# Weights converted from the first attention on, an output product behind the next norm, and norms half a pair ahead

**The chip, the cores and the metric.** One core of one Trainium2 chip. The metric is the device time of one execution in microseconds (us), the slowest core's, which is the only one here. All runs quoted are in the fast state. Kernels sent together ran on the same chip beside runs of the kernel before, and are compared with those.

## The reference

Eight sequences of 448 tokens: attention with 12 heads of 64 channels, q and k normed by their root mean square, then a feed-forward layer with SwiGLU over 768 channels and 1536 hidden units. Cut to what matters:

```python
q_n, k_n = rmsnorm(q, g_q), rmsnorm(k, g_k)
attn = softmax(q_n @ k_n.T / sqrt(64)) @ v            # 8 x 12 heads, 448 x 64
x  = attn.transpose(0, 2, 1, 3).reshape(3584, 768)
xn = x / sqrt(mean(x * x) + 1e-6) * rms_g
g  = xn @ w_gate
out = (g * sigmoid(g) * (xn @ w_val)) @ w_out         # weights come as 64-bit floats
```

## The kernel before

Two heads make a pair, six pairs a sequence, 48 pairs in all. One loop iteration `g` scores pair `g`, brings its exponentials to the values of pair `g - 1`, and transposes q and k of pair `g + 1`. (The code, and some of the recorded texts, call a transpose a turn too; in the text here a turn is a turn of the conversion, explained next.) TensorE (PE) fills the gaps of attention with the gate, value and output products of the sequence before. The product is a two by two block scheme with seven products, so sums of weight blocks are needed.

The weights come as 64-bit floats. A conversion **turn** takes one 128 x 384 block through ScalarE (ACT, two steps), GpSimd (POOL, a clamp), DVE (two integer steps) and GpSimd again (the join). The result is used by sequence 0 and stored for the other seven. There are 72 blocks, and a turn works on four of them in different steps:

```python
def split(raw):                       # turn n works on block n - 2 here
    nc.scalar.activation(top, hi, ACT.Abs)
    nc.scalar.activation(lo, lo, ACT.Copy, scale=2.0**-29)
    nc.gpsimd.tensor_scalar(top, top, 122879.99, 2.0**-15, ALU.min, ALU.max)      # the clamp
def join(lo, hi, top, dst):           # and on block n - 3 here
    nc.vector.tensor_scalar(top, top, 3, 0x3FFFFFF8, ...)                         # DVE step 1
    nc.vector.scalar_tensor_tensor(top, hi, -(2**30), top, ...)                   # DVE step 2
    nc.gpsimd.tensor_tensor(dst, top, lo, ALU.add)                                # the join
def convert():
    ... keep (store) what the turn before joined; join block n - 3;
    ... DVE subtractions for the sums of block n - 4; split block n - 2; load block n
```

The order of the loop body decides what each engine does in what order:

```python
for g in range(NG + 1):
    load_pair(g + 2)                  # q and k, on the same queue as the conversion's loads and stores
    pe(lambda: score(g, (0, 1)))
    squares(g + 2, 0)                 # ACT square; DVE sum one PE item later
    if solo: convert()                # solo: attention without products beside it (pairs 0 to 5)
    fill()                            # products, each followed by convert()
    pe(lambda: turn(g + 1, 0))
    ...
    squares(g + 2, 1)                 # two PE items later: GpSimd's root and q's norm
    pe(lambda: values(g - 1))         # bank ps_m
    load_v(g + 2)
    ...
    pe(lambda: sums(g - 1))           # DVE: reciprocal, then x = values * reciprocal, frees ps_m
    fill()
    pe(lambda: turn(g + 1, 1))        # bank ps_m again
    ...
```

`ps_m` is a single PSUM bank, shared by values and transposes; the scores have four banks and the products three.

Of the kernel before, what the change touches and what calls it, by code (L numbers as in the profile page):

```python
# [8 lines left out]
F32 = mybir.dt.float32  # L9
# [325 lines left out]
def safe_scores(  # L335
# [24 lines left out]

    RING, NH = 24, 14
    const, small = pool("c_const", 1), pool("c_small", 4)
    qk_pool, v_pool, qn_pool, qkT_pool = pool("c_qk", 3), pool("c_v", 3), pool("c_qn", 1), pool("c_qkT", 2)
    e_pool, tmp, y_pool = pool("c_e", 12), pool("c_tmp", 1), pool("c_y", 2)
    x_pool, s_pool, h_pool, w_pool = pool("c_x", 4), pool("c_xs", 3), pool("c_h", NH), pool("c_w", RING)
    raw_pool, cv_pool = pool("c_raw", 4), pool("c_cv", 2)
    scratch = pool("c_dram", 1, space=DRAM)
# [23 lines left out]
    def load_pair(g):  # L391
        if g >= NG:
            return
        b, hp = divmod(g, NPAIR)
        hs = slice(2 * hp, 2 * hp + 2)
        qk = st["qk", g] = qk_pool.tile([P, 2, 2 * NT * D], F32, name="qk")

        for h in range(2):
            nc.sync.dma_start(out=qk[:, 1].rearrange("p (t h d) -> p h t d", h=2, d=D)[:, h],  # L399
                              in_=k[b, 2 * hp + h].rearrange("(p t) d -> p t d", t=NT))  # L400
        nc.sync.dma_start(out=qk[:, 0].rearrange("p (h n) -> p h n", h=2), in_=q[b, hs].rearrange("h (p t) d -> p h (t d)", t=NT))

# [11 lines left out]
    def squares(g, i):  # L414

        if g >= NG:
            return
        n = 2 * NT
        if i == 0:
            st["ms", g] = small.tile([P, 2 * n], F32, name="ms")  # L420
        ms = st["ms", g]
        sq = tmp.tile([P, n * D], F32, name="sq", tag="sq", bufs=1)
        nc.scalar.activation(sq, st["qk", g][:, i], ACT.Square)  # L423

        def reduce():
            nc.vector.tensor_reduce(out=ms[:, i * n:(i + 1) * n], in_=sq.rearrange("p (n d) -> p n d", d=D), axis=AX_X, op=ALU.add)  # L426

        after(1, reduce)
        if i == 1:
            after(2, lambda: rms_qk(g))  # L430
            after(2, lambda: norm_q(g))

    def rms_qk(g):
        ms = st.pop(("ms", g))
        nc.gpsimd.tensor_scalar(ms, ms, 1.0 / D, 1e-6, ALU.mult, ALU.add)  # L435
        rs = st["rs", g] = small.tile([P, 4 * NT], F32, name="rs")
        nc.gpsimd.tensor_tensor(rs, ms, mhalf[0:P, :], ALU.pow)  # L437

# [58 lines left out]
    def sums(g):  # L497
# [25 lines left out]
        for c in range(NT):  # L523
            for j in range(2):
                st.pop(("e", g, c, j))
        for key in ("qk", "v", "qkT", "rs"):
            st.pop((key, g))
# [13 lines left out]
    def norm_x(b):  # L541
# [5 lines left out]
        for hp in range(NPAIR):  # L547
            x = st["x", b, hp // 3][:, hp % 3, :]
            nc.vector.scalar_tensor_tensor(x, x, rg[:, hp:hp + 1], ps[:, 0:S], ALU.mult, ALU.mult)

        a = st["left", b] = {f"A{r + 1}{h + 1}": st["x", b, h][:, :, r * HT:(r + 1) * HT] for r in range(2) for h in range(2)}
        for h in range(2):
# [20 lines left out]

    made = []

    def block():
        t = h_pool.tile([128, 512], F32, name="h")[:, 0:BW] if len(made) < NH else w_pool.tile([128, BW], F32, name="wt")
        made.append(False)
        return t, len(made) - 1

    def room(n):

        return all(made[i - RING] for i in range(len(made), len(made) + n) if i - RING >= NH)

# [38 lines left out]
    def keep(key):  # L623
        t = st[key][0]
        if key[0] == "wo":
            nc.sync.dma_start(out=kept_o[key[3], key[2]], in_=t)  # L626
        else:
            nc.sync.dma_start(out=kept[key[2], ORDER.index(key[3]), key[4]], in_=t)

    def convert(upto=None):  # L630
# [7 lines left out]
        if 0 <= n - 3 < len(pieces):  # L638
            key = pieces[n - 3][0]
            st[key] = block()  # L640
            join(*st.pop(("cv", n - 3)), st[key][0])
            if "B12" not in key:
                store.append(key)
        if 0 <= n - 4 < len(pieces) and pieces[n - 4][0][0] == "w":
            _, _, fp, name, w = pieces[n - 4][0]
            sums = {"B12": (("T1", "B12", "B11"), ("T2", "B22", "T1"), ("T3", "B22", "B12")), "B21": (("T4", "B21", "T2"),)}
            for to, plus, minus in sums.get(name, ()):
                key = ("w", 0, fp, to, w)
                st[key] = block()
                nc.vector.tensor_tensor(st[key][0], st["w", 0, fp, plus, w][0], st["w", 0, fp, minus, w][0], ALU.subtract)  # L650
                store.append(key)
            if name == "B12":
                made[st.pop(pieces[n - 4][0])[1]] = True
        if 0 <= n - 2 < len(pieces):
# [13 lines left out]
    def used(key):  # L668

        made[st.pop(key)[1]] = True  # L670
        upto = min(at_use[key] + 1 + AHEAD, len(uses))
        while asked["n"] < upto and room(1) and turn_of["n"] == len(pieces) + 5:
            key = uses[asked["n"]]
            asked["n"] += 1
            t, i = st[key] = block()
            nc.sync.dma_start(out=t, in_=kept_o[key[3], key[2]] if key[0] == "wo" else kept[key[2], ORDER.index(key[3]), key[4]])


    def product(b, fp, left, right, onto=None):
# [3 lines left out]
        for w in range(2):  # L683
            wt = st["w", b, fp, right, w][0]
            for c in range(3):
# [5 lines left out]
    def quad(b, fp):  # L691
# [33 lines left out]
        def p2():  # L725
            product(b, fp, "A12", "B21", onto=bank["a"])
            for fc in (fp, fp + NFP):
                st["h", b, fc] = h_pool.tile([128, 512], F32, name="h")
                if b % 2:

                    nc.gpsimd.tensor_copy(st["h", b, fc][:, 0:64], st.pop(("h", b - 1, fc))[:, S - 64:S])
            hand(bank["a"][:, 0:HT], bank["a"][:, HT:S], rows(fp)[:, 0:HT])
# [24 lines left out]
    def project_out(b, n, i, part, last):  # L757
# [5 lines left out]
        for fc in range(part * each, (part + 1) * each):  # L763
            nc.tensor.matmul(ps, lhsT=st["h", b, fc][:, i * 128:(i + 1) * 128], rhs=st["wo", b, n, fc][0],  # L764
                             start=(fc == 0), stop=(fc == NFC - 1))
            if last:
                used(("wo", b, n, fc))
        if part < OUT_PARTS - 1:
            return
# [13 lines left out]

    def ffn_items(b):

        items = []
        for fp in range(NFP):
            items += [(6 * HT, 8 * (fp + 1) + 5, fn) for fn in quad(b, fp)]
        tiles = 3 + b % 2
        for n in range(2):  # L790
            for i in range(tiles):
                for part in range(OUT_PARTS):
                    items.append((NFC // OUT_PARTS * HALF, 8 * NFP + NFC * (n + 1) + 4,
                                  lambda a=(b, n, i, part, i == tiles - 1): project_out(*a)))
        return items


    AHEAD, LEFT, SLOTS = 20, 7, 27
    todo, part = [], {"all": 0.0, "spent": 0.0, "slot": 0}

    def fill(n=None):

        if n is None:
            part["slot"] += 1
            upto = part["all"] * min(part["slot"] / SLOTS, 1.0)
            n = 0
            while n < len(todo) and part["spent"] + todo[n][0] / 2 < upto:
                part["spent"] += todo[n][0]
                n += 1
        for _ in range(n):  # L810
            if not todo:
                pe(idle)
                continue
            _, turns, fn = todo.pop(0)
# [7 lines left out]

    def begin(b):
        items = ffn_items(b)
        part.update(all=float(sum(c for c, _, _ in items[:-LEFT])), spent=0.0, slot=0)
        todo.extend(items)


    for g in range(2):
        load_pair(g)  # L830
    for g in range(2):
        load_v(g)
    ident = const.tile([128, 128], F32, name="ident")
    make_identity(nc, ident)
    ones = const.tile([128, D], F32, name="ones")
    nc.vector.memset(ones, 1.0)
    mhalf = const.tile([128, 4 * NT], F32, name="mhalf")
    nc.gpsimd.memset(mhalf, -0.5)
    gq = const.tile([128, 1], F32, name="gq")
    gk = const.tile([128, 1], F32, name="gk")  # L840
    for a in range(2):
        rows = slice(a * D, (a + 1) * D)
        nc.scalar.dma_start(out=gq[rows, :], in_=g_q.rearrange("(p o) -> p o", o=1))
        nc.scalar.dma_start(out=gk[rows, :], in_=g_k.rearrange("(p o) -> p o", o=1))
    rg = const.tile([128, NDC], F32, name="rg")
    nc.scalar.dma_start(out=rg, in_=moe_rms_g.rearrange("(c p) -> p c", p=128))
    row = const.tile([1, 2, D], F32, name="row")
    nc.scalar.dma_start(out=row[:, 0, :], in_=g_q.rearrange("(o d) -> o d", o=1))
    nc.scalar.dma_start(out=row[:, 1, :], in_=g_k.rearrange("(o d) -> o d", o=1))
    gqk = const.tile([128, 1], F32, name="gqk")  # L850
# [13 lines left out]
    squares(0, 1)  # L864
    pe(idle)
    squares(1, 0)
    pe(idle)
    squares(1, 1)
    pe(lambda: turn(0, 1))
    bound()  # L870
    pe(lambda: turn(0, 0))
    for g in range(NG + 1):
        b, hp = divmod(g, NPAIR)
        load_pair(g + 2)
        solo = alone(g)
        if g < NG:
            pe(lambda: score(g, (0, 1)))
        squares(g + 2, 0)
        if solo:
            convert()  # L880
# [3 lines left out]
        if solo:  # L884
            pe(lambda: turn(g + 1, 1))
        squares(g + 2, 1)
        if g:
            pe(lambda: values(g - 1))
        load_v(g + 2)
        if solo:  # L890
# [4 lines left out]
        if solo:  # L895
            convert()
            continue
        end = hp == 0
        fill(2 if end else None)
# [4 lines left out]
        if end:  # L904
# [4 lines left out]
            fill(len(todo))  # L909
            begin(b - 1)  # L910
        fill()
    fill(len(todo))
    pe(idle)
    pe(idle)
    pe(idle)

# [37 lines left out]
```

## Time and profile before

The median was 1782.95 us. The prediction below shows the windows and the main waits; two more waits are needed later. Columns: engine, waiting line, releaser, then us in total, times and the longest.

```profile
DVE top L604 <- POOL top L599: 60.5, 42, 3.7
...
PE tr L454 <- issue: 12.2, 3, 4.5
```

The first is DVE standing for the clamp before its first step. The second is a transpose on TensorE that waits for nothing that the profile names; by its place I read it as a wait for the free `ps_m` bank (such waits are gone in the run below that gives it another bank).

### The profile page before, as it was taken

Reading aid. Unit: us, or ns where it says so; the run is one execution under the profiler, and the core shown is the slowest. Engines: PE = TensorE matmul, PEld = TensorE weight load, DVE = VectorE, ACT = ScalarE, POOL = GpSimd, SP = SyncE. Lnnn points to the kernel's source line nnn. Section 1 sums busy time; section 2 is a strip of 40 time slices with the busy share of each in tenths; the row PEclk is TensorE's granted clock in tenths of the full one; section 3 lists DMA queues with packets and bytes.
Section 4 is the critical chain, followed back from the end, with each engine's and each line's share of the span. In section 5 each row is a group of like instructions: output and inputs, shape, how many; then the busy total and the mean of one; then the engine's idle time right before and its main releaser. Section 6 shows DMA issues by size and latency. Waiting matters only on the chain.

```text
span 1778.6 us, 21555 instructions
## 1 busy us (share of the span) xinstructions
PE 1679.7 (94%) x7688; PEld 1207.5 (68%) x7688; DVE 728.7 (41%) x1078; ACT 487.3 (27%) x945; POOL 670.4 (38%) x643
## 2 busy tenths in 40 slices
PE   5869777889999999999999999999999999999998
PEld 2337566458875688758885588757885588858975
DVE  2756766544341344324442344324442244323320
ACT  5634344423222223222322232322322222210100
POOL 4665666653333334342333333432433323311000
PEclk9879888899999999999999999999999999999999
DMA  5624565646443445336542355325542264426521
GB/s 134 195 92 133 190 194 182 196 135 200 128 127 94 142 147 151 93 104 193 155 132 87 94 161 165 113 92 185 159 140 73 88 187 137 124 71 190 175 81 46
DMA packets 224841, 243.77 MB, mean 137 GB/s; under 512 B 63957, under 2 KB 221653, under 8 KB 224725
## 3 DMA queue, kind: packets, MB, share of 16 engines
q1 hardware_dynamic: 223616, 242.30, 44.3%
q8 instruction: 63, 1.03, 0.2%
q14 instruction: 54, 0.43, 0.1%
q10 hardware_dynamic: 1108, 0.00, 0.0%
HBM read 209.98 MB, written 32.24 MB: 136 GB/s over the span
## 4 chain that ended last, share of the span: by engine, by line
PE 79%; ACT 0%; DMA 0%; SPq 0%; issue 0%; DVE 0%; ACTq 0%; POOL 0%
PE ff L686 38%; PE ff L764 23%; PE sc L469 7%; PE av L494 7%; PE den L506 2%; PE tr L454 1%; PE rb L545 0%; PE msx L535 0%; ACT qkT L457 0%; DMA qk<-in_q_dram 0%; SPq L399 0%; DVE y L774 0%; ACT top L597 0%; ACT raw L598 0%; SPq L626 0%
## 5 line engine op out<-in xcount | busy, mean ns | idle before, releaser
L686 PE MATMUL ff<-x,wt 128*128 128x224 f32 x2268 | 469.5, 360 | 19.3 <-ACT p L719 17.5
L686 PEld LDWEIGHTS ff<-x,wt 128*128 128x128 f32 x2268 | 431.7, 194 | 52.5 <-issue 39.4
L764 PE MATMUL ff<-wt,h 128*128 128x384 f32 x1344 | 455.7, 492 | 7.6 <-DVE h L709 4.4
L764 PEld LDWEIGHTS ff<-wt,h 128*128 128x128 f32 x1344 | 250.0, 191 | 195.6 <-issue 27.5
L686 PE MATMUL ff<-xs,wt 128*128 128x224 f32 x1692 | 348.9, 356 | 3.5 <-DVE cc L698 3.5
L686 PEld LDWEIGHTS ff<-xs,wt 128*128 128x128 f32 x1692 | 316.3, 191 | 29.3 <-issue 16.4
L473 ACT ACTIVATE e<-sc,rs 112x448 f32<-112x448 f32 x384 | 212.2, 635 | 248.3 <-PE sc L469 237.5
L483 POOL TENSOR_TENSOR es<-es,e 112x448 f32<-112x448 f32 x168 | 189.7, 1140 | 234.4 <-ACT e L473 227.9
L510 DVE RECIPROCAL rd<-den 128x448 f32<-128x448 f32 x48 | 141.9, 2956 | 137.5 <-PE den L506 137.5
L494 PE MATMUL av<-e,vt 112*64 112x448 f32 x768 | 165.6, 576 | 16.4 <-ACT qkT L457 14.0
L469 PE MATMUL sc<-qkT 64*112 64x448 f32 x768 | 173.3, 569 | 0.7 <-ACT qkT L457 0.7
L479 POOL TENSOR_TENSOR es<-e 112x448 f32<-112x448 f32 x84 | 96.6, 1171 | 179.8 <-ACT e L473 179.8
L437 POOL TENSOR_TENSOR rs<-ms,mhalf 112x16 f32<-112x16 f32 x48 | 140.2, 2921 | 4.0
L426 DVE TENSOR_REDUCE ms<-sq 112x8 f32<-112x512 f32 x96 | 65.3, 680 | 184.5 <-ACT sq L423 184.2
L494 PEld LDWEIGHTS av<-e,vt 112*64 112x64 f32 x768 | 54.0, 144 | 105.3 <-issue 88.6
L469 PEld LDWEIGHTS sc<-qkT 64*112 64x112 f32 x768 | 62.3, 175 | 78.0 <-issue 68.8
L435 POOL TENSOR_SCALAR ms<-ms 112x16 f32<-112x16 f32 x48 | 10.2, 212 | 278.4 <-DVE ms L426 277.4
L698 DVE TENSOR_TENSOR cc<-ff,u 128x448 f32<-128x448 f32 x96 | 59.8, 623 | 132.2 <-PE ff L686 132.0
L606 POOL TENSOR_TENSOR wt<-top,raw 128x384 int32<-128x384 int32 x64 | 68.6, 1071 | 92.8 <-DVE top L605 29.5
L522 POOL TENSOR_TENSOR ss<-ss,rd 128x448 f32<-128x448 f32 x40 | 46.3, 1158 | 119.1 <-ACT rd L521 119.1
L423 ACT ACTIVATE sq<-qk 112x512 f32<-112x512 f32 x96 | 60.6, 631 | 61.9 <-DMA qk<-in_q_dram 54.1
L698 DVE TENSOR_TENSOR u<-ff,u 128x448 f32<-128x448 f32 x48 | 29.9, 623 | 106.1 <-PE ff L686 106.1
(67 smaller groups left out, 1073.1 us busy)
## 6 DMA issues: line engine op xcount, KB each, us to landing
wt<-kept SPq DMA_DIRECT2D x588, 192.0 KB, 3.3
wt<-kept_o SPq DMA_DIRECT2D x168, 192.0 KB, 2.5
kept<-wt SPq DMA_DIRECT2D x72, 192.0 KB, 2.3
qk<-in_k_dram SPq DMA_DIRECT2D x96, 112.0 KB, 3.1
qk<-in_q_dram SPq DMA_DIRECT2D x48, 224.0 KB, 3.2
vt<-in_v_dram SPq DMA_DIRECT2D x48, 224.0 KB, 2.7
raw<-in_moe_w_gate_dram SPq DMA_DIRECT2D x24, 384.0 KB, 3.9
raw<-in_moe_w_val_dram SPq DMA_DIRECT2D x24, 384.0 KB, 3.6
```

The costliest lines, as they stand in the source:

```text
L426: nc.vector.tensor_reduce(out=ms[:, i * n:(i + 1) * n], in_=sq.rearrange("p (n d) -> p n d", d=D), axis=AX_X, op=ALU.add)
L437: nc.gpsimd.tensor_tensor(rs, ms, mhalf[0:P, :], ALU.pow)
L469: nc.tensor.matmul(ps[0:P, 0:S], lhsT=qkT[r, 1, c * P:(c + 1) * P], rhs=qkT[r, 0, :], start=True, stop=True)
L473: nc.scalar.activation(e, ps[0:P, 0:S], ACT.Exp, scale=rs[:, n:n + 1])
L479: nc.gpsimd.tensor_tensor(es, st["e", g, 0, j], st["e", g, 1, j], ALU.add)
L483: nc.gpsimd.tensor_tensor(es, es, st["e", g, c, j], ALU.add)
L494: nc.tensor.matmul(av[j * D:(j + 1) * D, 0:S], lhsT=vt[:, j, c, :], rhs=st["e", g, c, j], start=(c == 0), stop=(c == NT - 1))
L510: nc.vector.reciprocal(rd, den[:, 0:S])
L606: nc.gpsimd.tensor_tensor(dst.bitcast(I32), top, lo, ALU.add)
L686: nc.tensor.matmul(bank[:, w * HT:(w + 1) * HT], lhsT=wt[:, c * 128:(c + 1) * 128], rhs=x[:, c, :], start=onto is None and w == c == 0, st ...
L698: nc.vector.tensor_tensor(add[name], ps[:, 0:S], add[other], ALU.add)
L764: nc.tensor.matmul(ps, lhsT=st["h", b, fc][:, i * 128:(i + 1) * 128], rhs=st["wo", b, n, fc][0], start=(fc == 0), stop=(fc == NFC - 1))
```

## The change

The intent was to win from the time that TensorE loses before 397 us (the prediction puts it at 128 us): to start conversion with the first attention, to spread its turns one behind each product, to have norms ready earlier, and to give the norm between two sequences something to hide behind. Its core:

```diff
+    free_w = [slots.tile([128, BW], F32, name=f"w{i}") for i in range(NW)]     # a list of free places
     def room(n):
-        return all(made[i - RING] for i in ...)          # a ring: freed in order only
+        return len(free_w) + max(len(free_h) - 4, 0) >= n
-    raw_pool, cv_pool = pool("c_raw", 4), pool("c_cv", 2)
+    raw_pool, cv_pool = pool("c_raw", 4), pool("c_cv", 3)
...
+    def out_items(b): ...
     def begin(b, slots):
-        items = ffn_items(b)                             # gate and value, then output product
+        items = (out_items(b - 1) if b else []) + gate_value_items(b)
...
     squares(0, 1)
+    pe(lambda: turn(0, 1))
+    convert()
+    convert()
...
-        solo = alone(g)                                  # pairs 0 to 5
+        solo = g <= NPAIR                                # pairs 0 to 6
         load_pair(g + 2)
         pe(lambda: score(g, (0, 1)))
         squares(g + 2, 0)
+        squares(g + 2, 1)
...
-        squares(g + 2, 1)
         if g: pe(lambda: values(g - 1))
+        if g == NPAIR + 1: pe(lambda: rms_x(0))          # the first seam
```

At the start a dummy square draws the table load forward, q is loaded before k, and pair 0's roots are computed in two halves.

> **What bounds the kernel now.** I read the windows view first, cut at the places where the program changes its work: start, attention alone (pairs 0 to 5), the first seam (norm of sequence 0), gate, value and output products of sequence 0 beside attention and weight conversion, the rest.
>
> ```profile
> 0.00:15.00 15.00, 1.98 (x8) 1.32 (x8) 4.09 (x11) 4.25 (x6) 6.32 (x12) 1.00 0.70 179
> 15.00:97.00 82.00, 68.09 (x306) 27.74 (x308) 47.68 (x64) 52.46 (x101) 50.57 (x48) 0.90 0.54 160
> 97.00:137.00 40.00, 25.25 (x96) 14.55 (x96) 22.14 (x28) 9.70 (x18) 21.56 (x19) 0.70 0.23 72
> 137.00:397.00 260.00, 212.47 (x908) 150.21 (x907) 160.39 (x254) 103.35 (x209) 166.19 (x175) 0.91 0.54 171
> 397.00:1778.00 1381.00, 1371.92 (x6375) 1013.67 (x6374) 494.38 (x725) 317.56 (x613) 425.73 (x391) 1.00 0.43 131
> ```
>
> After the window, the columns are PE, weight loads, DVE, ACT, POOL, then granted clock. From 397 us on TensorE is busy 99% at full clock and nothing can be won but matmuls; the change removes none. Before 397 us, PE is idle 89 us and its clock is reduced.
>
> I priced the work by start-to-start times of the later timeline: a gate/value product of 12 matmuls 2.28 us, an output item of 8 matmuls 2.60, an attention pair 9.06 (1.69 + 1.69 scores, 3.1 values, 0.9 sums, 0.8 turns, switches), 2.3 more where the sums are on PE. Two sequences in the later part then cost 84 x 2.275 + 42 x 2.58 + 12 x 9.06 = 408 us, the period that the timeline has (811.25 to 1219.46). Work done by 397 us at that price: 12.5 pairs' parts, 42 products and 18 output items, some 268 us. **The loss is about 128 us**: 14 in the start, 24 in attention alone (82 - 58), 23 at the seam (40 - 17), 66 in the long window (260 - 194). That is the most that can be won.
>
> Who holds PE there? The waits of PE and ACT:
>
> ```profile
> PE tr L454 <- POOL qn L441: 22.1, 5, 7.0
> PE ff L686 <- ACT p L719: 17.5, 4, 5.9
> PE av L494 <- ACT qkT L457: 14.0, 9, 4.5
> ACT top L597 <- POOL wt L606: 86.7, 46, 4.9
> ACT sq L423 <- DMA qk<-in_q_dram: 54.1, 20, 3.9
> ```
>
> PE waits for the normed q, and for ACT copies that are themselves short. ACT is late because, in its order, each conversion's first step (L597) needs the top tile freed by POOL's last step (L606), 87 us in 46 waits. POOL's timeline in a burst shows the cause:
>
> ```profile
> 318.77 1.01 POOL L606 TENSOR_TENSOR wt<-top,raw 128x384 int32<-128x384 int32 x1 [1.22 <-DMA kept_o<-wt]
> 319.74 0.51 POOL L599 TENSOR_SCALAR top<-top 128x384 f32<-128x384 f32 x1
> 321.47 1.00 POOL L606 TENSOR_TENSOR wt<-top,raw 128x384 int32<-128x384 int32 x1 [1.22 <-DMA kept_o<-wt]
> ```
>
> One turn of the conversion is a serial chain: join 1.0, clamp 0.5, DVE's two steps 0.36 + 0.56 and the hand-overs: 321.47 - 318.77 = **2.70 us a turn**. There are 77 turns.
>
> **What the skill says.** "TensorE: Matmul & The Clock Gate", part 1, says that the clock falls to half after an idle window of about 3.4 us and returns after about as long of work. The trace agrees: after 5.89 us idle at 221.93 a product takes 4.39 us, against 2.43, and the granted clock of 220 to 240 us is 0.77. So each PE wait removed returns somewhat more than its length. The same page, section "Architectural detail", calls ACT, DVE and GpSimd strict FIFO; the late ACT copies above fit. "SBUF — State Buffer", "Who interferes with whom", says that a DVE tensor_tensor with both inputs in SBUF contends with GpSimd reads. The trace fits: such subtractions (L650) are 0.55 us at best and 0.80 on average. "ScalarE: Activation LUTs", "What ACT_TABLE_LOAD costs", gives 1283 ns; the trace has 1283.
>
> **The change part by part.** I walked both programs' emission order and counted turns (c), with no time in it.
>
> (1) Start. The dummy Square draws the table load (1.28 us, now at 5.00 behind seven ACT DMA issues) before the data; q is loaded first; pair 0's roots are split, so that q's root has 8 columns. From 16 columns 2.92 and 4 columns 1.02 I estimate 1.65 for 8. q lands about 5, square 0.63, reduce 0.69, POOL 0.2 + 1.65 + 1.04, turns 1.0, copy 0.63: first score near 11.5 in place of 15.2. Loss 14 becomes 10.5.
>
> (2) Attention alone now covers pairs 0 to 6. Turns reached: 22, against 18 at its end before; the list allows no more (34 usable blocks, less a margin of 4). POOL per pair: norms 4.15, ss 1.15, three turns 8.1, less what fits in chain gaps: about 12.5 us; DVE 10.4, PE 10.5. Both roots are emitted half a pair earlier, which removes the qn waits of this stretch (11.2 us). I put 24 us for pairs 0 and 1 (now 26), four of 12.5 (now 14 on average), 14 for pair 6, whose turns share the single ps_m bank: from 11.5 to 99 or so, say 97, against work of 67: loss 19 in place of 24, with a pair and four turns more done.
>
> (3) First seam, now in iteration 7. Same chain (ss add, matmul, root 1.02, matmul, six multiplications 3.64, differences 3.2), one qn wait of 3.9 gone: loss 16 in place of 23.
>
> (4) Sequence 0's products. Before, conversions come in bursts: 3 at each second-half fp, 5 before the output product, 3 in its middle, which PE waits out, since a ring slot frees only in order. Now a slot is taken from whatever is free: one turn follows each product, and the walk shows forced turns only at c62-63 and c73-75. With three top buffers ACT is one turn freer. What stays is POOL's chain. From the seam to the first product of sequence 1: 55 turns x 2.7 = 148, 7.3 pairs x 12.3 (norms 4.15, es adds 6.9, ss 1.15) = 90, less some 35 that fit in gaps, plus 21 for DVE's reciprocals and sums in the chain: **224 to 232 us**. PE's work in the same stretch: 40 x 2.28 + 18 x 2.6 + 7.3 x 9.06 = 204. So POOL stays the bound by a little: loss 28. The same sum for the kernel before gives 229 where 253 was measured; the 24 left over is the alternation of bursts and products, which goes.
>
> Sum of losses: 10.5 + 19 + 16 + 28 = 73.5, against 128: gain 54.
>
> (5) The seam in the later part. Now the last two products of a sequence lie behind the norm, and the output items follow. Three PSUM banks rotate: the first output item takes the bank that the last product still fills, so it waits for its addition on DVE, estimated 0.8 us; and the root has one product (2.3) in place of one output item (2.6) to hide behind, some 0.3. With 7 seams: **loss 7**. The end has more PE work without attention, at the same 100%. Total gain 47: 1783 - 47 = **1736**, which I round to 1737.
>
> **Rivals.** (A) POOL isn't the bound after all, the chain's gaps hold the attention work, and PE runs through: loss in part 4 about 10 and in part 2 about 13, time near 1713. For it: POOL is busy only 64% of 137 to 397. Against: 2.7 us a turn is serial, and POOL's order is unchanged. (B) The chain, not the bursts, is what was measured: 77 turns at the old pace of 3.9 us, output items (2.6 us each 2 turns' worth of chain) waiting in iteration 13, where ten parts meet 13 turns; then the gain is start, seam and one pair, 20 to 25 us: 1760. For it: DVE and POOL are both 62 to 64% busy already and slow each other. Against: PE's named waits there are ACT, at burst positions. (C) Both squares now stand together in ACT's order and may wait for a late k load, holding exps and turns in every iteration; plus seam waits over 3 us that drop the clock: 1775 to 1790. Against: the q load was issued last before, so the old first square already waited for all three loads; at most 3.9 us, and the later part has slack.
>
> **Range and chances.** Centre 1737; A and B lie about 24 us to both sides, so 8 in 10 between 1715 and 1762. The 2% line is 1747. B reaches beyond it, the centre doesn't: faster by over 2% 0.67, within 2% 0.32, slower 0.01.
>
> **What would show it.** First score at 11 to 12.5 us; the first product of sequence 0 near 120 and of sequence 1 near 360 in the timeline; PE waits for ACT p gone, ACT top waits for POOL wt under 30 us; POOL and DVE over 70% busy between; PE busy over 97% afterwards, with some 1 us before the first output item of each seam. Wrong if PE's idle time before sequence 1 stays above 80 us, or if the later part shows waits of several us at its seams.

## The result

The changed kernel took 1783.83 us (1782.27 to 1784.77, 4 runs) against 1783.18 us (1781.13 to 1784.4, 4 runs) of the kernel before in the same rounds: a ratio of 1.0004, 95% interval 0.9987 to 1.0021. **Nothing was won.** Ratios here and below are the mean time of one kernel's fast runs over that of the other's of the same rounds, so they differ a little from the ratio of the medians quoted. The outputs are correct.

The windows of the changed kernel, with the columns and the last four of the stretches that the prediction used for the kernel before (us, then PE, weight loads, DVE, ACT, POOL, granted clock, DMA share, GB/s):

```profile
15.00:97.00 82.00, 70.02 (x304) 28.68 (x304) 54.47 (x75) 52.86 (x105) 56.33 (x55) 0.92 0.61 190
97.00:137.00 40.00, 23.40 (x96) 9.21 (x96) 13.22 (x16) 10.83 (x21) 25.83 (x24) 0.74 0.29 84
137.00:397.00 260.00, 210.13 (x918) 149.36 (x919) 177.99 (x260) 106.33 (x215) 170.40 (x173) 0.91 0.50 154
397.00:1778.00 1381.00, 1374.03 (x6356) 1016.34 (x6354) 488.56 (x716) 309.08 (x594) 415.92 (x381) 1.00 0.44 132
```

The last row is as before. Between 137 and 397 us TensorE did 918 matmuls in place of 908. Cut instead where the program's own work changes (first score, head of iteration 7, second product of sequence 0, first product of sequence 1):

```profile
10.14:120.20 110.06, 85.25 (x362) 34.20 (x362) 61.42 (x88) 62.39 (x122) 73.40 (x72) 0.88 0.59 178
120.20:145.02 24.82, 18.27 (x75) 10.54 (x74) 16.23 (x19) 7.10 (x15) 11.58 (x10) 0.79 0.11 33
145.02:414.54 269.52, 220.88 (x962) 152.26 (x960) 174.84 (x251) 105.32 (x214) 174.60 (x175) 0.92 0.51 157
414.54:1781.30 1366.76, 1356.49 (x6290) 1007.67 (x6288) 483.88 (x712) 307.37 (x591) 411.72 (x378) 1.00 0.44 131
```

At the prediction's prices, the first row holds 67 us of work, the second a pair and two products (9.06 + 4.56), the third 204. So the losses are 43, some 11 and 65.5, with 10 for the start: **about 129 us, where 73.5 was predicted and 128 was there before.** Of the third row's 65.5 us, 48.6 are idle time of TensorE (269.5 less 220.9); the other 17 or so are work that took longer than priced, at a granted clock of 0.92. The last row needs care: the kernel before spends 1382 us after its first product of sequence 1, but has two pairs more to do there (it has done 208 of the score matmuls by then, the changed kernel 240, and a pair has 16). That is 16.4 us at the prediction's price of a pair without its switches (8.18) and 18.1 with them (9.06), so the later part of the changed kernel is 1 to 3 us longer.

The waits of the changed kernel:

```profile
ACT sq L423 <- DMA qk<-in_q_dram: 62.6, 21, 6.7
DVE top L621 <- POOL top L616: 60.8, 37, 5.4
ACT top L614 <- POOL w L623: 24.1, 10, 5.3
PE tr L460 <- issue: 20.3, 5, 8.7
PE tr L460 <- POOL qn L447: 11.8, 6, 4.2
PE ff L703 <- ACT p L736: 4.6, 1, 4.6
```

The waits that the prediction went after did fall: ACT for the join from 86.7 to 24.1, products for ACT from 17.5 to 4.6, transposes for the normed q from 22.1 to 11.8. In their place stand longer waits for the q load, and for the `ps_m` bank (20.3 against 12.2). DVE waits for the clamp as long as before.

### The profile page after: what moved, and what is told of

Its sections match the earlier page's. It is cut to its first block, busy times and chain, and to the rows that moved or that the text cites. A ratio compares the mean times of both kernels' runs of the same rounds, so it can differ in the third digit from the quotient of the medians.

```text
span 1781.3 us, 21585 instructions
## 1 busy us (share of the span) xinstructions
PE 1682.9 (94%) x7688; PEld 1206.0 (68%) x7688; DVE 739.9 (42%) x1078; ACT 486.8 (27%) x946; POOL 676.6 (38%) x645
## 3 DMA queue, kind: packets, MB, share of 16 engines
q8 instruction: 63, 1.03, 0.2%
## 4 chain that ended last, share of the span: by engine, by line
PE 78%; POOL 2%; ACT 1%; issue 1%; DMA 0%; DVE 0%; SPq 0%; ACTq 0%; POOLq 0%
PE ff L703 37%; PE ff L783 24%; PE av L500 6%; PE sc L475 6%; PE den L512 2%; PE tr L460 1%; POOL es L489 1%; PE rb L551 0%; POOL rs L545 0%; ACT e L479 0%; ACT qkT L463 0%; DMA qk<-in_k_dram 0%; DMA raw<-in_moe_w_out_dram 0%; ACT top L614 0%; DVE xs L566 0%
## 5 line engine op out<-in xcount | busy, mean ns | idle before, releaser
L703 PE MATMUL ff<-x,w 128*128 128x224 f32 x2256 | 470.5, 360 | 7.4 <-ACT p L736 4.6
L703 PEld LDWEIGHTS ff<-x,w 128*128 128x128 f32 x2256 | 424.2, 193 | 58.7 <-issue 32.1
L783 PE MATMUL ff<-w,h 128*128 128x384 f32 x1344 | 452.1, 492 | 5.5 <-DVE h L726 5.5
L783 PEld LDWEIGHTS ff<-w,h 128*128 128x128 f32 x1344 | 252.0, 191 | 191.9 <-issue 25.3
L703 PE MATMUL ff<-xs,w 128*128 128x224 f32 x1716 | 350.5, 354 | 3.5 <-DVE cc L715 1.9
L703 PEld LDWEIGHTS ff<-xs,w 128*128 128x128 f32 x1716 | 321.9, 190 | 12.7 <-issue 5.6
L489 POOL TENSOR_TENSOR es<-es,e 112x448 f32<-112x448 f32 x168 | 195.4, 1173 | 264.7 <-ACT e L479 258.1
L443 POOL TENSOR_TENSOR rs<-ms,mhalf 112x16 f32<-112x16 f32 (+1 forms) x49 | 141.6, 2890 | 4.1
L623 POOL TENSOR_TENSOR w<-top,raw 128x384 int32<-128x384 int32 x69 | 73.1, 1060 | 102.0 <-issue 29.7
L423 ACT ACTIVATE sq<-qk 112x512 f32<-112x512 f32 x96 | 57.8, 638 | 74.6 <-DMA qk<-in_q_dram 62.6
L795 DVE COPY y<-ff 128x384 f32<-128x384 f32 x24 | 13.3, 554 | 152.7 <-PE ff L783 152.7
```

Of the source, the lines that this page charges most:

```text
L443: nc.gpsimd.tensor_tensor(st["rs", g][:, cols], ms, mhalf[0:P, cols], ALU.pow)
L489: nc.gpsimd.tensor_tensor(es, es, st["e", g, c, j], ALU.add)
L623: nc.gpsimd.tensor_tensor(dst.bitcast(I32), top, lo, ALU.add)
L703: nc.tensor.matmul(bank[:, w * HT:(w + 1) * HT], lhsT=wt[:, c * 128:(c + 1) * 128], rhs=x[:, c, :], start=onto is None and w == c == 0, st ...
L783: nc.tensor.matmul(ps, lhsT=st["h", b, fc][:, i * 128:(i + 1) * 128], rhs=data(("wo", b, n, fc)), start=(fc == 0), stop=(fc == NFC - 1))
```

## The experiments

Seventeen kernels ran. To place a gain, I use two landmarks of the timeline: the start of the first product of sequence 0 (P0) and of sequence 1 (P1). In the changed kernel P0 is at 137.8 and P1 at 414.5 us, so P0 to P1 is 276.7, and the rest after P1 is 1366.8. That rest was between 1366.8 and 1368.2 us in every variant of the changed kernel that kept its order and was looked at, so everything below happens before P1.

### The ceiling: no conversion at all

The arithmetic and the 64-bit loads are taken out; each place is filled by a plain load (wrong on purpose).

```diff
-            join(*st.pop(("cv", n - 3)), data(key))
+            load_plain(n - 3, data(key))
-            st["cv", n - 2] = split(st.pop(("raw", n - 2)))
-            st["raw", n] = load_raw(pieces[n][1])
```

> The changed kernel with the conversion's arithmetic taken out (each block is filled by one plain load of other finite data; wrong result on purpose; stores, sums of weights, products and order kept). If the loss before sequence 1 (some 130 us in both kernels) is conversion work and its waits on ACT, DVE and POOL: first product of sequence 1 comes near 320 us in place of 414, and the time falls to 1690 to 1705. If it is the attention's own chain (norms, sums on POOL, one bank for turns and values): over 1750.

Measured: 1720.62 us, ratio 0.9643 (0.9627 to 0.9659). P0 is at 117.2 and P0 to P1 takes 234.8. So conversion costs the changed kernel 20 us before P0 and 42 between, and the place to look is right. The same edit on the kernel before:

> The kernel before with the conversion's arithmetic taken out as in e1 (wrong result on purpose). e1 came to 1721, so 63 us of the changed kernel's loss is conversion and some 67 is not. If conversion costs the kernel before more, as the prediction had it (bursts), and the rest is alike: about 1718 to 1725 here too, so the change has bought nothing on either count. If this comes clearly below 1715, the change has added waits of its own that have nothing to do with conversion; clearly above 1735, it has removed such.

It gave 1755.76 us, ratio 0.9846 (0.9828 to 0.9864), but isn't a clean ceiling: the plain load is asked for only at the join, and at the bursts of that kernel the engines wait for it to land (output products wait 8.8 us in 6 for such loads in its trace). The recorded expectation took over 1735 us as a sign that the change had removed waits that have nothing to do with conversion; with these loads in the way I draw nothing from it.

### Attention alone: the load queue

One round of the attention-only stretch, from the timeline of the changed kernel. First the queue that issues the loads and stores (start, us, queue, line, transfer), from one q load to the next:

```profile
84.89 0.48 SPq L397 DMA_DIRECT2D qk<-in_q_dram  x1
...
91.63 0.43 SPq L605 DMA_DIRECT2D raw<-in_moe_w_val_dram  x1
99.03 0.80 SPq L645 DMA_DIRECT2D kept<-h  x2
99.91 0.40 SPq L605 DMA_DIRECT2D raw<-in_moe_w_gate_dram  x1
100.37 0.53 SPq L397 DMA_DIRECT2D qk<-in_q_dram  x1
```

Then ACT, waiting for that q load, and GpSimd in the same round:

```profile
88.58 0.63 ACT L423 ACTIVATE sq<-qk 112x512 f32<-112x512 f32 x1 [5.30 <-DMA qk<-in_q_dram]
```

```profile
94.00 2.91 POOL L443 TENSOR_TENSOR rs<-ms,mhalf 112x16 f32<-112x16 f32 x1
96.99 1.04 POOL L447 TENSOR_TENSOR qn<-qk,rs 112x512 f32<-112x512 f32 x1
97.99 1.01 POOL L623 TENSOR_TENSOR h<-top,raw 128x384 int32<-128x384 int32 x1
```

It closes a circle of 15.5 us: q load at 84.89, square at 88.58, root at 94.00 and norm, then the join that stands behind them in GpSimd's order, then the store of a joined block at 99.03, and behind that store, in the queue's order, the next q load at 100.37. The queue was quiet from 92 to 99 us. The Trainium skill, "DMA: Bandwidth & Descriptors", section "Anatomy of one DMA — SWDGE (gpsimd) path", says that DMA engines don't wait on semaphores, and that the wait happens on the issuing sequencer before dispatch. (The section is about DMAs that GpSimd issues; these are issued by SyncE.) The trace agrees: the queue's own waits have, over the whole execution, 100.2 us in 25 for a join ahead of a store. A load with nothing to wait for is held by the store ahead of it. The test asks for q and k a pair earlier:

```diff
-        load_pair(g + 2)
+        load_pair(g + 3)          # and load_pair(2) before the loop
```

> The changed kernel with q and k loaded one pair earlier (pair g + 3 in place of g + 2 at the head of iteration g; same buffers). Theory 'load loop': the q and k loads stand in the SP queue behind raw loads that wait for POOL's join, POOL's join stands behind the norms, and the norms wait for the loads, 15.5 us around, which is the pace of attention alone (14.8 to 15.7 us a pair). Then ACT's 48 us of waits for the q load go, attention alone runs at 12 us a pair, and the time is 1745 to 1765. Theory 'conversion chain' (POOL and DVE hand each piece to and fro in order): the pace stays near 15 us, time over 1775.

Measured: 1767.75 us, ratio 0.9908 (0.9891 to 0.9924), against 1.0004 unedited: 17 us won. ACT's wait for q falls from 62.6 to 1.9 us, and P0 comes 13 us earlier, at 124.7. On the kernel before:

> The kernel before with q and k loaded one pair earlier, nothing else. ACT waits for the q load 24 us before 400 us there (48 in the changed kernel). If the load loop holds it too: 1765 to 1775. If the loop is what the change itself tightened: within 4 us of 1783.

1774.54 us, ratio 0.995 (0.9932 to 0.9967): 9 us. But in its trace P0 comes only 1.6 us earlier (128.3 against 129.9), and P0 to P1 is 3.9 us shorter, so in that kernel the late load cost little of the attention-only stretch. The circle as the limit of that stretch is shown for the changed kernel alone.

### Pair 6 alone: one bank

The changed kernel gives pair 6 to the attention-only stretch too, but the transposes in that iteration (those of pair 7) are in the single bank `ps_m`, which the values use too. That iteration took 26 us. In the changed kernel's timeline of TensorE:

```profile
108.15 1.01 PE L460 MATMUL tr<-ident,qk 112*128 112x112 f32 x4 [9.42 <-ACT qkT L463]
```

The transpose of k waits 9.42 us for ACT's copy of the transpose of q out of the same bank; ACT itself stood for a q load. Using the then idle product banks:

```diff
-        ps = (ps_f if alone(g - 1) else ps_m).tile(...)
+        ps = (ps_f if g - 1 <= NPAIR else ps_m).tile(...)
```

> The changed kernel with the turns of pair 7, which stand in the last iteration of attention alone, in the three ff banks (unused there) in place of the single bank that turns and values share. Theory 'single bank': the 9.4 us wait of the k turn for the q turn's copy in that iteration goes, and the time falls by 6 to 10 us, 1774 to 1778. If ACT is late there only because it waits for the q load (6.7 us just before), the wait moves to the next instruction and the time stays within 3 us of 1784.

1778.77 us, ratio 0.9972 (0.9955 to 0.9989): 6 us, P0 at 131.3. The opposite cure is to leave pair 6 out of the stretch, as before:

```diff
-        solo = g <= NPAIR
+        solo = g < NPAIR          # the first seam goes back to the general one
```

> The changed kernel with attention alone for pairs 0 to 5 only and sequence 0's products begun after the seam of iteration 6, as before; 21 turns done there; everything else of the change kept. Theory: the extra pair alone (26 us for 9.7 us of matmuls, against 15 for the others) cost what the start and the spreading won; then this is 8 to 15 us faster, 1769 to 1776. Rival: the time is set by the conversion's pace, so that where the products begin does not matter: within 4 us of 1784.

1794.18 us, ratio 1.0061 (1.0043 to 1.0078): slower by 10 us. P0 comes 8 us earlier, at 129.9, but P1 comes 8 us later, at 423.0. So the extra pair isn't what cost the gain. Why it is worth its time stays open: at P0 that run has only one conversion turn fewer behind it (22 raw loads asked for, against 23), and the edit also moves the seam into the general order of the loop. Between P0 and P1 it has at most one pair more to do (half a pair's scores, one pair's values), 9 us or less; at least 7 of the 16.4 us more are not explained.

### Products of sequence 0: were the bursts a cost?

The prediction's step 4 says that bursts of turns cost 24 us, beside the turns themselves. Bring bursts back:

```diff
             pe(fn)
-            convert()
+            if turns > 8 * NFP + 5:       # only behind output items
+                convert()
```

> The changed kernel with one line of the change's effect undone: a gate or value product is no longer followed by a conversion turn of its own, so turns come in bursts of 7 or 8 before the first product of each block and 11 before the output product, as in the kernel before or worse. The prediction's step 4 said that such bursts alone cost about 24 us of the loss beside the products of sequence 0. Theory of the prediction (bursts cost time of their own): 1800 us or more, with TensorE standing at the bursts. Rival (the sum of DVE's and GpSimd's work and their in-order waits for one another set the pace of this stretch, so the placing of the turns in it is nearly free): within 6 us of the changed kernel's 1784, and the idle time of TensorE before sequence 1's first product stays at about 130 us.

1839.46 us, ratio 1.03 (1.028 to 1.032). P0 to P1 is 333.9, 57 us more, and TensorE stands at the bursts, as the waits of TensorE show:

```profile
PE ff L703 <- DVE w L667: 44.6, 8, 11.8
```

These bursts (7 or 8 turns) are larger than those of the kernel before, so 57 is no measure of what those cost. But the rival, that placing is free, has fallen: **spreading the turns is worth time against such bursts**. That something else in the change takes it back is the guess that the next runs test.

### What took it back: the early norms

```diff
         squares(g + 2, 0)
-        squares(g + 2, 1)
         ...
+        squares(g + 2, 1)                 # back where it was
         if g: pe(lambda: values(g - 1))
```

> The changed kernel with the k square of pair g+2 back where it was, half an iteration later (the root and q's norm follow it). If emitting the norms half a pair ahead is worth what the prediction's step 2 took for it (11 us of GpSimd waits), the time rises by 5 to 12 us, to 1789 to 1796. If instead the round that sets the pace of the attention-only stretch is q load, square, reduction, root, join, kept store, next q load, then asking for the norms half a pair earlier only makes ACT and DVE stand earlier for a load that isn't there, and the time is unchanged or falls: 1776 to 1784.

1769.14 us, ratio 0.9911 (0.9891 to 0.993): 17 us better **without** this part of the change. P0 hardly moves (138.5 against 137.8); P0 to P1 falls from 276.7 to 261.8. The traces of the two kernels show how. In the changed kernel, GpSimd and then DVE:

```profile
280.64 2.91 POOL L443 TENSOR_TENSOR rs<-ms,mhalf 112x16 f32<-112x16 f32 x1
283.63 1.04 POOL L447 TENSOR_TENSOR qn<-qk,rs 112x512 f32<-112x512 f32 x1
284.63 1.00 POOL L623 TENSOR_TENSOR w<-top,raw 128x384 int32<-128x384 int32 x1
285.60 0.51 POOL L616 TENSOR_SCALAR top<-top 128x384 f32<-128x384 f32 x1
```

```profile
286.14 0.36 DVE L621 TENSOR_SCALAR top<-top 128x384 int32<-128x384 int32 x1 [3.05 <-POOL top L616]
286.53 0.56 DVE L622 SCALAR_TENSOR_TENSOR top<-raw,top 128x384 int32<-128x384 int32 x1
287.01 0.55 DVE L667 TENSOR_TENSOR w<-w,w 128x384 f32<-128x384 f32 x1
287.48 2.95 DVE L516 RECIPROCAL rd<-den 128x448 f32<-128x448 f32 x1
290.46 0.62 DVE L523 TENSOR_TENSOR x<-av,rd 128x448 f32<-128x448 f32 x1
```

And TensorE:

```profile
291.19 0.98 PE L460 MATMUL tr<-ident,qk 112*128 112x112 f32 x4 [8.73 <-issue]
```

Root and norm hold GpSimd for 4 us; the clamp comes behind them; DVE stands 3.05 us for the clamp, in front of a reciprocal that doesn't need it; the values' bank is read only at 290.46; and the transpose of k, which needs that bank, has waited 8.73 us. With the k square at its old place, at the same point of the program, the reciprocal goes first and the root runs beside it (DVE, GpSimd, TensorE):

```profile
278.23 2.95 DVE L516 RECIPROCAL rd<-den 128x448 f32<-128x448 f32 x1
281.21 0.62 DVE L523 TENSOR_TENSOR x<-av,rd 128x448 f32<-128x448 f32 x1
```

```profile
279.43 2.91 POOL L443 TENSOR_TENSOR rs<-ms,mhalf 112x16 f32<-112x16 f32 x1
```

```profile
281.94 0.98 PE L460 MATMUL tr<-ident,qk 112*128 112x112 f32 x4 [6.93 <-issue]
```

At this one point the wait of the transpose is only 1.8 us shorter, 6.93 against 8.73. The gain is in the sum: between P0 and P1 such waits fall from 20.3 us in 5 to 9.7 in 3, and DVE's waits for the clamp from 42.2 to 31.7 us. So some 10.6 of the 15 us are this wait.

Is this general, or only so where each product has its turn? The mirror puts this one part into the kernel before (with a second buffer for the square, without which, by the recorded expectation, the order deadlocks; no run tried that):

```diff
         squares(g + 2, 0)
+        squares(g + 2, 1)
         ...
-        squares(g + 2, 1)
```

> The kernel before with this one part of the change: both squares at the head of an iteration (and a second buffer for the square, without which the order deadlocks). If norms half a pair ahead cost time wherever conversion turns are under way, because DVE's reciprocal comes to stand behind a clamp that stands behind the norm chain, this is 5 to 15 us slower than before, 1788 to 1800. If the cost needs a turn behind each product, as only the changed kernel has it, the kernel before only loses its waits for the normed q (22 us in 5 waits): 1768 to 1780.

1796.27 us, ratio 1.0066 (1.0049 to 1.0083): 12 us slower. Between the two profiled executions 15.8 us lie: 4.6 are lost by the first product of sequence 0 (134.5 against 129.9), 7.6 from there to the first of sequence 1, 3.6 after it. So it costs in both kernels.

### And the order of the output product

```diff
-        items = (out_items(b - 1) if b else []) + gate_value_items(b)
+        items = gate_value_items(b) + out_items(b)
```

> The changed kernel with each sequence's output product back behind its own gate and value products, before the next norm. The prediction's step 5 took 7 us of loss at the later seams for the new order; the traces show none (1366.8 us for the rest after, against 1382 before less the 16 us of two attention pairs already done). If it was worth nothing either way later, only the products of sequence 0 change: their 28 output turns then have to be done before the second seam, with fewer products to spread them over, which I put at 5 to 20 us more: 1788 to 1804. If the new order did cost at the seams, or holds up the turns, the time falls to 1770 to 1780.

1776.84 us, ratio 0.9952 (0.9935 to 0.9969): 9 us better than with the new order by the ratios, 5 by the two profiled spans (1776.5 and 1781.3). P1 comes at 391.6, with two pairs (16.4 to 18.1 us) fewer done than in the changed kernel; so 4 to 6 us of the cost lie before P1, while conversion still runs. The rest after it, 1384.9 us with those pairs to do, is 0 to 2 us longer with the old order: within the price of a pair, level.

### DVE's share of the conversion

```diff
-        nc.vector.tensor_scalar(top, top, 3, 0x3FFFFFF8, ...)
-        nc.vector.scalar_tensor_tensor(top, hi, -(2**30), top, ...)
```

> The changed kernel without DVE's two integer steps of each conversion (77 turns x (0.56 + 0.36) us = 71 us of DVE's time and one hand-over between GpSimd and DVE each way; wrong results on purpose; loads, stores and GpSimd's clamp and join stay). If DVE standing in its own order for GpSimd's clamp (59 us in 36 waits), and its load with it, sets the products of sequence 0, this wins most of the 42 us that removing the whole conversion won there: 1735 to 1755. If GpSimd's own work (1.5 us a turn plus norms) is the bound, as the prediction's sum said, only the hand-overs go: 1765 to 1780. The attention-only stretch should keep nearly its pace of some 15 us a pair, for its round goes over GpSimd's join and the load queue.

1742.04 us (wrong on purpose), ratio 0.9759 (0.9738 to 0.978). P0 is unchanged (136.7), and P0 to P1 is 234.4 us, the same as without any conversion (234.8), though GpSimd is as busy in that stretch as ever (175.1 us, against 174.6). GpSimd's own work therefore isn't the bound: it fits beside TensorE. What binds is DVE's part: its work, and that it hands back and forth. P0 to P1 of the changed kernel, and the same without DVE's steps (window, us, then PE, weight loads, DVE, ACT, POOL, granted clock, DMA share, GB/s):

```profile
137.83:414.54 276.71, 227.67 (x985) 158.03 (x985) 181.83 (x262) 108.04 (x219) 174.60 (x175) 0.91 0.50 153
136.67:371.10 234.43, 214.76 (x985) 150.43 (x985) 127.73 (x156) 106.77 (x219) 175.06 (x175) 0.97 0.58 180
```

On the kernel before:

> The kernel before without DVE's two integer steps of each conversion (wrong results on purpose; the mirror of the run that did this to the changed kernel and gave 41 us). If the same bound, DVE's work and its waits in order, holds the products of sequence 0 in both kernels, the gain is of the same size: 1740 to 1755. If in the kernel before it was the one step from GpSimd's join to ACT's next copy (86 us of waits) and the bursts that held TensorE, as the prediction read it, the gain is under 20 us: 1763 to 1780.

1748.96 us, ratio 0.9805 (0.9788 to 0.9821): 35 us. There, 26 us come from P0 to P1 (240.4 against 266.7). The recorded expectation allowed under 20 us if ACT's waits for the join and the bursts, as the prediction read it, held that kernel. But the edit shortens those waits too: they fall from 86.7 to 15.8 us, since a join that need not wait for DVE comes sooner. So this run shows that DVE's steps stand in the way in both kernels, and not by which wait in the kernel before.

How much of it is hand-over, and how much sheer work? The next edit keeps all the work, and gives each hand-over between GpSimd and DVE one turn more (one buffer more of each kind):

```diff
-        if 0 <= n - 3 < len(pieces): ... join(block n - 3)    # DVE's steps and the join in one turn
+        if 0 <= n - 4 < len(pieces): ... join(block n - 4)    # the join, a turn later
+        if 0 <= n - 3 < len(pieces): mix(*st["cv", n - 3])    # DVE's steps, behind it
-    raw_pool, cv_pool = pool("c_raw", 4), pool("c_cv", 3)
+    raw_pool, cv_pool = pool("c_raw", 5), pool("c_cv", 4)
```

> The changed kernel with the conversion pipeline one turn deeper: DVE's two steps of a piece are issued a turn after POOL's clamp, POOL's join a turn after DVE's steps, so no engine waits in its queue for the step just issued (one more top and raw buffer). Theory 'conversion chain': DVE's 59 us of waits for the clamp shrink under 20, POOL's waits before the join too, a burst takes 1.6 us a turn in place of 2.7, and the time is 1740 to 1760. Theory 'load loop': time within 10 us of 1784, since POOL's order of join and norm is the same.

1770.66 us, ratio 0.9924 (0.9907 to 0.9941): 14 us. DVE's wait for the clamp falls from 60.8 us to 26.4, and P0 to P1 to 261.1. So about 16 of the 42 us are waits in order that one turn more removes; the remainder needs a look at how long DVE's work takes. The same subtraction (line 667 in the changed kernel, between P0 and the second seam) takes 971 ns on average there, 989 without DVE's two steps but with GpSimd's, and 636 without conversion. In the view of one line, DVE's first step (minimum, median and maximum in ns) has:

```profile
L621 DVE TENSOR_SCALAR top<-top x72: 343/359/1293, 12.8 to 386.9; 128x384 int32<-128x384 int32 x72
```

The long ones have the length of the short one plus one GpSimd instruction of about 1 us; that they stood for one is my inference. The prediction quoted the skill's page on this contention for the subtractions, and put nothing on it in its sum.

### Together, and a version that beats both

Early loads, product banks for pair 6 and the deeper conversion:

> The changed kernel with the three edits of e2 (q and k one pair earlier, -16 us), e3 (deeper conversion, -13) and e4 (turns of pair 7 in other banks, -5) together. If each takes away a separate wait: the sum, 1750. If they wait for the same thing (a chain of queues in which only the slowest link counts), the second edit adds little: 1762 to 1768. If each alone only moved the wait to the next link, together they give more than the sum: under 1745.

1749.08 us, ratio 0.9805 (0.9787 to 0.9822). The separate gains (17, 14, 6) add up to 37; 35 are there. In what is left, the waits of the k transpose for the bank lead (20.6 us in 3). So, on top:

```diff
+        where, tag = (ps_f, "f") if g - 1 <= NPAIR else (ps_m, "m") if i == 0 else (ps_s, "s")
```

> The version with the three edits together (1749 us) with one more: from pair 8 on, the transposes of k go to the banks of the scores in place of the one bank that values, sums and the transposes of q share. If that one bank couples TensorE to DVE in what is left of the products' loss (k turns that wait 4 to 8 us), 1735 to 1744, which is over 2% under both kernels. If the score banks are then short for the exponentials, or the waits were only a symptom of ACT's and DVE's late copies, 1747 to 1756.

1739.9 us, ratio 0.9745 (0.9727 to 0.9763). P0 to P1 goes from 261.8 to 252.1, and no transpose waits for a bank any more. With this base I undid the two parts that had cost time. First the norms:

> The four edits together (1740 us) with the k square back at its old place too. If asking for the norms early costs time because GpSimd's root and norm (4.4 us) then run ahead of a clamp that DVE waits for in front of its reciprocal and value scaling, the deeper conversion has already cut that wait (42 us in 26 waits to 12 in 6) and this edit is worth little here: 1736 to 1744. If the norm chain's place matters by itself, the 15 us of the changed kernel come again in part: 1725 to 1734.

1749.32 us, ratio 0.9802 (0.9785 to 0.9818): **slower** by 10. P0 to P1 is 253.2, as with the early norms (252.1), so here early norms cost nothing there. Two links of the chain above are gone in this base, most of DVE's waits for the clamp (12.0 us in 6 are left) and the bank's wait; which of the two it takes was not tested apart. But P0 comes at 127.2 in place of 119.0: with the loads out of the way, early norms are worth 8 us in the attention-only stretch. Both of my expectations had missed that. Then the output product:

> The four edits together (1740 us, early norms kept) with the output product back before the next norm, which won 7 us in the changed kernel (5 us less beside the products of sequence 0, some 2 us lost later). If that gain came from the forced turns and the waits at the second seam, which the four edits leave in place (waits of 2.6 us for the root and 5.2 us for the first output item), it should come again: 1732 to 1737. If it came from a wait that the deeper conversion and the other bank already removed, the time is 1738 to 1746.

**1729.11 us, ratio 0.97 (0.9684 to 0.9717), correct: 3% under both kernels.** The gain of the old order came again, so it doesn't hang on the waits that the four edits removed. It lies before P1 here too: P0 to P1 is 224.7 us with two pairs fewer done, which makes 241 to 243 against 252.1. What in that order costs the time was not tested. Its window over the products of sequence 0:

```profile
137.00:397.00 260.00, 239.93 (x1099) 178.53 (x1099) 186.93 (x257) 104.42 (x211) 170.10 (x171) 0.97 0.62 189
```

That is 1099 matmuls in 260 us, where the changed kernel did 918.

## Why the prediction was wrong, point by point

The predicted sum of losses was 73.5 us before sequence 1's products plus 7 later; it is 129, and 1 to 3 later. That gains and losses came to nothing in the end is a coincidence of this kernel, no law.

**Step 1, the start, was right.** First score at 10.14 (estimated 11.5); the root of 8 columns took 1.66 us (estimated 1.65).

**Step 2, attention alone, failed:** a loss of 19 was predicted, 43 came. It added up POOL, DVE and PE per pair and took the largest sum, "about 12.5 us" a pair. The first two pairs took the 24 us that it gave them. The next four took 14.0, 14.8, 15.7 and 15.4 us, 60 in place of 50, as the heads of iterations 2 to 6 stand at 34.3, 48.3, 63.1, 78.8 and 94.2. The circle through the load queue isn't in any engine's sum; early loads won 13 us of it. Rival C had named the late load, but put it at 3.9 us. Pair 6 was priced at 14 us with its one bank in mind, and took 26; 6.5 of these are shown to be the bank. (Its own parts add up to 99 us; "say 97" took 2 us off without a reason.)

**Step 3, the seam, was right and rather too careful:** a loss of some 11 against 16.

**Step 4, the products, failed:** 28 predicted, 65.5 measured. Its claim that bursts cost time was borne out for the larger bursts of one run. The step that failed is "what stays is POOL's chain", 224 to 232 us in a stretch that took 269.5. Two things were wrong in it. The first is what stands behind what: the sum took POOL's work as movable into gaps ("less some 35"), while the change itself moved 4 us of root and norm in front of a clamp that DVE awaits before its reciprocal. Putting that back won 15 us here, and the new output order cost 4 to 6. The prediction had counted the early norms as a pure gain.

The second is the bound. The 2.70 us a turn did hold DVE's two steps, but only as links of a serial chain. If the chain were all, the run that takes the hand-overs apart and keeps the work would have reached TensorE's 204: with join and clamp alone in the chain, 1.5 us a turn, the same sum gives 55 x 1.5 + 90 - 35 + 21 = 158 (my estimate, from the prediction's terms). It won 15.6 us. Taking DVE's steps out won 42. So DVE's own work, busy 174.8 us in that stretch, has to have a line of its own in the sum. How much of it is contention with GpSimd was not separated.

By themselves the early norms cost 17 us and the output order 9, by the ratios. That these two gave back what the rest of the change had won is argued from these two runs: they were not undone together in the changed kernel.

I don't claim that the 65.5 us are fully divided: the separate edits overlap, and what the bursts of the kernel before cost by themselves was not measured, only that larger ones cost 57.

**Step 5 was wrong in place:** of the 7 us of loss at the later seams 1 to 3 came in all, and none of it is shown to be the new order's; that lost 4 to 6 us before P1, where conversion was still running.

**The rivals.** C was nearest: its 1775 to 1790 us hold the 1783.8, and it blamed the two squares standing together, which did cost 17 us. Its way was another, though: a late k load that holds ACT. ACT's waits for k came to 9.1 us in 15, none over 0.8; the time went through the root and norm that follow the squares. B, the smaller gain, had 1760 and the wait of output items for turns. "DVE and POOL are both busy and slow each other", its argument, should have had a number.

**The marks.** It had written that it is wrong if TensorE's idle time before sequence 1 stays above 80 us; the sign came (88 us before 397). Of the marks for the steps, the first score, the fallen ACT waits and the busy later part (1374 of 1381 us) came; POOL and DVE at over 70% only nearly (66 and 68% of 137 to 397); the first products came at 138 and 415, not 120 and 360.

## What to carry to other kernels

Where an engine works through its queue in order, an instruction moved earlier is paid by everything behind it: before moving one, write down the next few entries of that queue, who waits for each, and which bank or buffer that waiter holds. On the queue of this kernel a load was issued only after the stores ahead of it, which set the pace at 15.5 us a pair; so on a queue that carries both, ask for it a whole period earlier rather than place it better. And test a change's parts one at a time: here two of them cost time by themselves, and one of the two became a gain once other waits were gone.

## What the Trainium skill lacked or had wrong

- "SBUF — State Buffer", "Who interferes with whom" is right in kind: DVE's first step, a tensor_scalar, took 343 ns at best and 1293 at worst, the subtraction of two SBUF tensors 546 to 2344, and tensor_reduce, which the page says never contends on trn2, 664 to 687 (that the long ones stood for GpSimd is inferred). It lacks what this comes to in a mixed stretch: the subtraction's mean was 971 ns, against 636 with the whole conversion gone.
- No page that I found gives the cost of a power on GpSimd by its columns: 1.02 us for 4, 1.66 for 8 and 2.91 for 16, at 112 partitions. It is the longest entry of the norm chain here.
- "DMA: Bandwidth & Descriptors" has the rule for where a DMA waits, but not its consequence for a queue that mixes loads with stores: here 15.5 us a pair, with the queue silent for 7 of them in the round shown.
